# Another seven-product form for the second matmul of groups 1 to 5: four chained sums a side, products gathered in three banks

## Chip, cores and metric

The kernel runs on one core of one Trainium2 chip. The time is device time in microseconds of one execution; beside it stands the span, the time from the first to the last instruction in the profile of one execution. The core's engines are TensorE (PE in the profile; its weight loads are PEld), VectorE (DVE), ScalarE (ACT), GpSimd (POOL) and SyncE (SP, which here only issues DMAs).

## What is computed

The input is `q`, `k`, `v` of 4 batches, 8 heads, 768 positions and 64 channels. A linear attention with a decay for each head is worked out block by block. Its output, seen as 3072 tokens of 512 channels, goes through an MLP: a matmul with `w_in`, an exact GELU, a matmul with `w_out`.

```python
for b in range(nb):                                  # blocks of 64 positions
    intra = einsum('bhic,bhjc->bhij', qb, kb) * Dmask
    intra = einsum('bhij,bhjd->bhid', intra, vb)
    inter = einsum('bhid,bhde->bhie', qb * lam_pow, kv_state)
    out[:, :, sl] = intra + inter
    kv_state = lam_block * kv_state + einsum('bhsd,bhse->bhde', kb * rev_pow, vb)
h = x @ w_in                                         # 3072 x 512 by 512 x 2048
g = 0.5 * h * (1 + erf(h / sqrt(2)))
return g @ w_out                                     # 3072 x 2048 by 2048 x 512
```

## The kernel before

The 3072 tokens are worked on in six groups of 512, four chunks of 128 tokens each. For every group the attention gives `x_t`, the first matmul (`mm1`, L511 to L522) multiplies it with `w_in` into PSUM tiles `h_ps`, and ACT writes the GELU of each as bf16 into `g_t`, with the 2048 hidden channels on partitions in 16 slices `k` and the 512 tokens in the free dimension. The second matmul takes `g_t` and `w_out_t`, both bf16. Group 0 does it plainly (`mm2`, L526). Groups 1 to 5 do it in `blocks_by_seven` (L375): `g_t` is cut in two halves of the tokens (`lo`, `hi`) and two of the hidden channels (slices 0 to 7 and 8 to 15), `w_out_t` in two halves of the hidden channels and two of the output channels (B11, B12, B21, B22), and the 2 by 2 block product, eight products by definition, is made of seven.

The seven-product form before needs five sums of blocks of `w_out_t`, made once while group 0 runs (`w_out_sums`, L371, ten DVE instructions at L368), and five sums of blocks of `g_t` for each group (`g_sum`, L384, ten DVE instructions at L389, half of each issued inside the first matmul, blocks 10 to 14 of the group, the other half inside the second). Each product is worked out in two parts `u` of 128 tokens; one part is eight matmuls of 128 weights by 256 columns into one half of a PSUM tile of 128 x 2 x 256 f32 (L414). One such tile fills one PSUM bank. The products run in the order `m3 m4 m5 m2 m1 m6 m7`. Products 3 and 4 are copied to SBUF by ACT (L433, L443). DVE adds or subtracts the others with them (L452, L453, L465, L466, L484, L489, L498; in group 5 L482 and L495 by halves of 256 columns). Product 7 is added on top of product 1 in the same bank `r_ps`, and that bank is read after both halves of product 1 and again after product 7. In group 5 each half of `r_ps` is a tile of its own. The results are stored from `o0_sb` (the first two chunks) and `o1_sb` (the last two) by SP (`store`, L421).

PSUM tiles come from rings by tag: `mo` and `mh` have two banks each. `mh` also holds `h_ps`, and `mo` also holds the `kv_ps` of the attention.

The order is written by hand. A group of 1 to 5 is a list of 30 blocks, 16 of the first matmul and 14 of the second (L501), each of equal cost, and the steps of the attention for later groups are put in front of blocks by their number (`steps`, where `B` is one block, and `g + 26 * B` is block 26 of group `g`). Each engine runs its instructions in the order in which they were issued. The steps that fall among the last blocks of the second matmul are the two `empty_half` (L333, a DVE multiplication from the attention's PSUM to `x_t`; in groups 1 to 4, before blocks 26 and 28) and, in groups 1 to 3, four DMA transposes of `k` and `q` on SP's queue before block 26. Group 1 has more: a visit of the attention before block 20 that takes both banks of `mh`, a mask and states for it, and four ACT copies before block 23 (`reorder_states`, L229).

Of the kernel before, what the change touches and what calls it, by code (L numbers as in the profile page):

```python
# [8 lines left out]
F32 = mybir.dt.float32  # L9
BF16 = mybir.dt.bfloat16  # L10
ALU = mybir.AluOpType
# [4 lines left out]
def kernel(  # L16
# [10 lines left out]
    nc = tc.nc  # L27

    B, H, S, D = q.shape
    d_model, d_ff = moe_w_in.shape  # L30
# [21 lines left out]
    out_pool = ctx.enter_context(tc.tile_pool(name="outp", bufs=2))  # L52
# [36 lines left out]
    w_out_t = w_pool.tile([128, NK2, d_model], BF16)  # L89
# [58 lines left out]
    def bank(shape, dtype, tag, name):  # L148
        return ps.tile(shape, dtype, tag=tag, name=name, bufs=2 if tag in ("sc", "mh", "mo") else 1)
# [191 lines left out]
    def empty_outputs(c):  # L341
# [6 lines left out]
        else:  # L348
# [3 lines left out]
    KH = NK2 // 2  # L352
    DH = d_model // 2
    wsum = {}
    w_lo, w_hi = slice(0, KH), slice(KH, NK2)
    d_lo, d_hi = slice(0, DH), slice(DH, d_model)
    B11, B12, B21, B22 = ((w_lo, d_lo), (w_lo, d_hi), (w_hi, d_lo), (w_hi, d_hi))
    W_SUMS = {1: (B11, B22, ALU.add), 3: (B12, B22, ALU.subtract), 4: (B21, B11, ALU.subtract),
              6: (B11, B12, ALU.add), 7: (B21, B22, ALU.add)}

    def w_out_sum(i, half):

        if i not in wsum:
            wsum[i] = w_pool.tile([128, KH, DH], BF16, name=f"w_sum{i}")
        (ka, da), (kb, db), op = W_SUMS[i]
        n = KH // 2
        at = lambda ks: slice(ks.start + half * n, ks.start + (half + 1) * n)
        nc.vector.tensor_tensor(wsum[i][:, half * n:(half + 1) * n, :], w_out_t[:, at(ka), da], w_out_t[:, at(kb), db],  # L368
                                op=op)

    def w_out_sums():  # L371
        for i, half in [(6, 0), (6, 1), (7, 0), (1, 0), (3, 0), (4, 0), (7, 1), (1, 1), (3, 1), (4, 1)]:
            w_out_sum(i, half)

    def blocks_by_seven(g, g_t, first):  # L375

        last = g == NG - 1
        TH = M * C // 2
        lo, hi = slice(0, TH), slice(TH, 2 * TH)
        gsum = {}  # L380
        G_SUMS = {6: (0, hi, 0, lo, ALU.subtract), 1: (0, lo, KH, hi, ALU.add), 2: (0, hi, KH, hi, ALU.add),
                  5: (0, lo, KH, lo, ALU.add), 7: (KH, lo, KH, hi, ALU.subtract)}

        def g_sum(i, k):  # L384
            if i not in gsum:
                gsum[i] = sum_pool.tile([128, KH, TH], BF16, tag=f"g{i}", name=f"g_sum{i}")
            ka, ta, kb, tb, op = G_SUMS[i]
            ks = slice(k, k + n4)
            nc.vector.tensor_tensor(gsum[i][:, ks, :], g_t[:, ka + k:ka + k + n4, ta], g_t[:, kb + k:kb + k + n4, tb],  # L389
                                    op=op)  # L390

        n4 = KH // 2

        def with_sums(i, run):
            def both():
                run()
                if i in sums_at:
                    g_sum((5, 2, 1, 6, 7)[sums_at.index(i)], 0)
            return both

        sums_at = range(10, 15)
        blocks = [(with_sums(i, run), cost) for i, (run, cost) in enumerate(first)]

        left = {1: lambda k, t: gsum[1][:, k, t], 2: lambda k, t: gsum[2][:, k, t],
                3: lambda k, t: g_t[:, k, t], 4: lambda k, t: g_t[:, KH + k, TH + t.start:TH + t.stop],
                5: lambda k, t: gsum[5][:, k, t], 6: lambda k, t: gsum[6][:, k, t], 7: lambda k, t: gsum[7][:, k, t]}
        right = {2: lambda k: w_out_t[:, k, d_lo], 5: lambda k: w_out_t[:, KH + k, d_hi]}
        right.update({i: (lambda k, i=i: wsum[i][:, k, :]) for i in W_SUMS})

        banks, sb = {}, {}  # L410

        def product(i, u, o, begin):
            for k in range(KH):
                nc.tensor.matmul(o, left[i](k, slice(u * C, (u + 1) * C)), right[i](k),  # L414
                                 start=(begin and k == 0), stop=(k == KH - 1), skip_group_check=True)

        def tile_f(name):
            sb[name] = sum_pool.tile([128, 2, DH], F32, tag=f"f_{name}", name=f"f_{name}")
            return sb[name]

        def store(rows, us, cols):  # L421
            b = slice(rows * 2 + us.start, rows * 2 + us.stop)
            dst = out_r[g, :, b, cols]
            nc.sync.dma_start(dst, sb["o0" if rows == 0 else "o1"][:, us, cols])

        both, every = slice(0, 2), slice(0, d_model)

        def m3(u):
            if u == 0:
                banks["p"] = bank([128, 2, DH], F32, "mo", "p_ps")  # L430
            product(3, u, banks["p"][:, u, :], u == 0)
            if u == 1:
                nc.scalar.copy(tile_f("e"), banks["p"])  # L433
                g_sum(5, n4)

        def m4(u):
            if u == 0:
                banks["q"] = bank([128, 2, DH], F32, "mo", "q_ps")
            product(4, u, banks["q"][:, u, :], u == 0)
            if u == 0:  # L440
                g_sum(2, n4)
            else:
                nc.scalar.copy(tile_f("f"), banks["q"])  # L443

        def m5(u):
            if u == 0:
                banks["p5"] = bank([128, 2, DH], F32, "mo", "p5_ps")
                g_sum(1, n4)
            product(5, u, banks["p5"][:, u, :], u == 0)
            if u == 1:  # L450
                sb["o0"] = out_pool.tile([128, 2, d_model], F32, tag="o0", name="o0_sb", bufs=1)
                nc.vector.tensor_add(sb["o0"][:, :, d_hi], sb["e"], banks["p5"])  # L452
                nc.vector.tensor_sub(tile_f("x1"), sb["f"], banks["p5"])  # L453
                if last:
                    store(0, both, d_hi)

        def m2(u):
            if u == 0:
                banks["q2"] = bank([128, 2, DH], F32, "mo", "q2_ps")
            product(2, u, banks["q2"][:, u, :], u == 0)  # L460
            if u == 0:
                g_sum(6, n4)
            else:
                sb["o1"] = out_pool.tile([128, 2, d_model], F32, tag="o1", name="o1_sb", bufs=1)
                nc.vector.tensor_add(sb["o1"][:, :, d_lo], sb["f"], banks["q2"])  # L465
                nc.vector.tensor_sub(tile_f("x2"), sb["e"], banks["q2"])  # L466

        def m1(u):
            if u == 0:
                banks["s"] = bank([128, 2, DH], F32, "mh", "s_ps")  # L470
                if last:
                    banks["r"] = [bank([128, DH], F32, tag, "r_ps") for tag in ("mh", "t")]
                else:
                    r_ps = bank([128, 2, DH], F32, "mh", "r_ps")
                    banks["r"] = [r_ps[:, 0, :], r_ps[:, 1, :]]
                    banks["r_all"] = r_ps
            product(1, u, banks["r"][u], u == 0 or last)
            if u == 0:
                g_sum(7, n4)
            elif last:  # L480
                for w in range(2):
                    nc.vector.tensor_add(sb["x2"][:, w, :], sb["x2"][:, w, :], banks["r"][w])  # L482
            else:
                nc.vector.tensor_add(sb["x2"], sb["x2"], banks["r_all"])  # L484

        def m6(u):
            product(6, u, banks["s"][:, u, :], u == 0)
            if u == 1:
                nc.vector.tensor_add(sb["o1"][:, :, d_hi], sb["x2"], banks["s"])  # L489
                store(1, both, every)  # L490

        def m7(u):
            product(7, u, banks["r"][u], False)
            if last:
                nc.vector.tensor_add(sb["o0"][:, u, d_lo], sb["x1"][:, u, :], banks["r"][u])  # L495
                store(0, slice(u, u + 1), d_lo)
            elif u == 1:
                nc.vector.tensor_add(sb["o0"][:, :, d_lo], sb["x1"], banks["r_all"])  # L498
                store(0, both, every)

        blocks += [((lambda f=f, u=u: f(u)), KH * DH) for f in (m3, m4, m5, m2, m1, m6, m7) for u in range(2)]  # L501
        return blocks

    N1 = 19
# [79 lines left out]
    def early(n):  # L584
        live[n] = begin(n, early=True)
        return live[n]
# [10 lines left out]
    c = early(0)  # L597
# [7 lines left out]
    c = early(1)  # L605
# [48 lines left out]
    e = N1  # L654
# [22 lines left out]
    def at(when, run):  # L677
        todo.append((place(when), run))
# [103 lines left out]
    n = 2 * M  # L782
# [9 lines left out]
    for g in range(2, NG):  # L792
        n = (g + 1) * M
# [14 lines left out]
        w = g + (10 if g == 2 else 8) * B  # L808
# [7 lines left out]
    for g in range(1, NG - 2):  # L816
        n = (g + 2) * M
# [48 lines left out]
```

## Time and profile before

| what | us |
| --- | --- |
| median of three executions | 202.98 |
| lowest, highest of the three | 200.58, 205.71 |
| the profiled execution | 201.34 |
| its span | 199.6 |
| outside the span | 1.74 |
| second matmul, group 1 | 67.06 to 80.95 |
| second matmul, group 2 | 98.25 to 110.47 |
| second matmul, group 3 | 127.82 to 140.05 |
| second matmul, group 4 | 156.48 to 168.71 |
| second matmul, group 5 | 183.57 to 195.8 |
| busy DVE, ACT over the span | 120.4, 82.7 |

A row of the profile's groups reads: line, engine, operation, output<-input, shape, count, then busy time in us, mean duration of one in ns, and the engine's idle time before them with what ended it. A row of the timeline reads: start in us, duration in us, engine, line, operation, count, and in brackets the idle time before it with what ended it. A row of the chain of work that ended last reads: start in us, duration, engine and line. Matmuls overlap in the array: a chain of sixteen lasts 1.91 us in the timeline from its first start to its last modelled end, and the next chain starts 1.75 us after it.

### The profile page before, as it was taken

The page shows a single profiled execution, that of the slowest core. Times are in us where ns is not written, and L with a number is a line of the kernel's source. Part 1 is how long each engine was busy: PE and PEld are TensorE (multiplying, and loading weights), DVE is VectorE, ACT ScalarE, POOL GpSimd, SP SyncE. Part 2 cuts the span into 40 slices and gives each one's busy share as a digit, 9 for nine tenths or more (in the row PEclk, how much of TensorE's full clock was granted, in tenths as well). Part 3 has the DMA queues.
Part 4 walks back from the last instruction along what each step waited for, and adds up shares of the span by engine and source line. Part 5 has one row for each costly group of instructions (what it writes and reads, how often), then busy time and mean ns, then how long its engine had stood idle before and what let it go on. Part 6 is the DMA issues. An engine that isn't in the chain of part 4 may idle for free.

```text
span 199.6 us, 5998 instructions
## 1 busy us (share of the span) xinstructions
PE 191.0 (96%) x2625; PEld 142.9 (72%) x2636; DVE 120.4 (60%) x206; ACT 82.7 (41%) x149; POOL 110.5 (55%) x136
## 2 busy tenths in 40 slices
PE   7699999999999999999999989999999999999992
PEld 2388674455887788885688875688884788865881
DVE  3753507764473869694949658649638358341482
ACT  4964564234556413174520255520355410566200
POOL 8999973499969799993493497591400000000000
PEclk9999999999999999999999999999999999999999
DMA  5999999999999999999799799899700002300014
GB/s 115 148 174 175 200 204 206 153 216 150 130 220 149 151 142 136 118 209 233 72 84 153 234 68 127 90 110 122 234 8 3 3 0 80 134 0 3 0 53 158
DMA packets 102761, 24.76 MB, mean 124 GB/s; under 512 B 93264, under 2 KB 99920, under 8 KB 102736
## 3 DMA queue, kind: packets, MB, share of 16 engines
q0 software_dynamic: 81072, 13.38, 99.3%
q1 hardware_dynamic: 21664, 11.02, 26.6%
q8 instruction: 20, 0.33, 0.7%
q14 instruction: 5, 0.04, 0.1%
HBM read 27.27 MB, written 6.29 MB: 168 GB/s over the span
## 4 chain that ended last, share of the span: by engine, by line
PE 73%; DMA 10%; POOL 10%; DVE 4%; issue 1%; POOLq 0%; DVEq 0%
PE h_ps L518 35%; PE r_ps L414 8%; PE p_ps L414 8%; PE q_ps L414 8%; DMA q_t<-in_q_dram 6%; DMA w_out_t<-in_moe_w_out_dram 4%; PE s_ps L414 4%; POOL w_in_t L94 3%; PE o_ps L531 3%; POOL k_t L70 2%; POOL q_t L70 2%; POOL v_t L70 2%; PE o_ps L314 2%; POOL v_dec L160 1%; PE kv_ps L290 1%
## 5 line engine op out<-in xcount | busy, mean ns | idle before, releaser
L518 PE MATMUL h_ps<-x_t,w_in_t 128*128 128x256 bf16 (+3 forms) x648 | 87.5, 290 | 1.0 <-issue 0.6
L521 ACT ACTIVATE g_t<-h_ps 128x512 bf16<-128x512 f32 (+2 forms) x99 | 57.8, 584 | 72.6 <-PE h_ps L518 72.6
L518 PEld LDWEIGHTS <-w_in_t 128*128 128x128 bf16 x656 | 58.4, 98 | 23.8 <-issue 1.0
L389 DVE TENSOR_TENSOR g_sum<-g_t 128x1024 bf16<-128x1024 bf16 x50 | 33.4, 713 | 16.4 <-ACT g_t L521 16.4
L414 PEld LDWEIGHTS <-g_sum 128*128 128x128 bf16 x400 | 39.1, 98 | 4.8 <-issue 0.3
L160 POOL TENSOR_TENSOR v_dec<-v_t,lam_m 128x512 bf16<-128x512 bf16 x23 | 24.3, 1094 | 25.6 <-PE o_ps L326 14.8
L70 POOL DMA_DIRECT2D v_t<-in_v_dram x24 | 22.2, 927 | 3.1 <-DMA w_out_t<-in_moe_w_out_dram 1.7
L414 PE MATMUL r_ps<-w_sum,g_sum 128*128 128x256 bf16 x160 | 19.1, 273 | 0.1
L73 POOL DMA_DIRECT2D k_t<-in_k_dram x24 | 18.7, 799 | 0.0
L73 POOL DMA_DIRECT2D q_t<-in_q_dram x24 | 18.3, 788 | 0.0
L414 PEld LDWEIGHTS <-g_t 128*128 128x128 bf16 x160 | 15.6, 98 | 2.9
L531 PE MATMUL o_ps<-w_out_t,g_t 128*128 128x512 bf16 x61 | 14.5, 379 | 0.4 <-issue 0.3
L333 DVE TENSOR_TENSOR x_t<-o_ps,lam_q 128x512 bf16<-128x512 f32 x16 | 10.6, 683 | 3.9 <-PE o_ps L314 3.9
L70 POOL DMA_DIRECT2D k_t<-in_k_dram x12 | 11.2, 933 | 1.9 <-DMA w_out_t<-in_moe_w_out_dram 1.6
L70 POOL DMA_DIRECT2D q_t<-in_q_dram x12 | 10.9, 908 | 2.4 <-DMA w_out_t<-in_moe_w_out_dram 2.4
L531 PEld LDWEIGHTS <-g_t 128*128 128x128 bf16 x64 | 5.9, 98 | 6.3
L305 DVE TENSOR_TENSOR sc_m<-sc_ps,cmask_d 128x512 bf16<-128x512 f32 x16 | 10.3, 679 | 0.0
L452 DVE TENSOR_TENSOR o_sb<-f_e,p_ps 128x512 f32<-128x512 f32 x5 | 3.4, 686 | 11.0 <-issue 11.0
L582 PE MATMUL idle_ps<-idle 128*128 128x256 bf16 (+1 forms) x40 | 8.7, 353 | 1.2 <-DVE idle L107 1.2
L414 PE MATMUL p_ps<-w_out_t,g_sum 128*128 128x256 bf16 x80 | 9.6, 273 | 0.0
L414 PE MATMUL s_ps<-w_sum,g_sum 128*128 128x256 bf16 x80 | 9.6, 273 | 0.0
L414 PE MATMUL q_ps<-w_out_t,g_sum 128*128 128x256 bf16 x80 | 9.6, 273 | 0.0
(90 smaller groups left out, 192.2 us busy)
## 6 DMA issues: line engine op xcount, KB each, us to landing
out_dram<-o_sb SPq DMA_DIRECT2D x9, 512.0 KB, 4.9
v_t<-in_v_dram POOLq DMA_DIRECT2D x24, 128.0 KB, 5.6
w_out_t<-in_moe_w_out_dram POOLq DMA_DIRECT2D x4, 512.0 KB, 10.3
w_in_t<-in_moe_w_in_dram POOLq DMA_DIRECT2D x7, 256.0 KB, 7.3
k_t<-in_k_dram POOLq DMA_DIRECT2D x12, 128.0 KB, 6.5
q_t<-in_q_dram POOLq DMA_DIRECT2D x12, 128.0 KB, 6.8
k_t<-in_k_dram POOLq DMA_DIRECT2D x24, 64.0 KB, 4.8
q_t<-in_q_dram POOLq DMA_DIRECT2D x24, 64.0 KB, 5.0
```

The source lines that it names most:

```text
L70: nc.gpsimd.dma_start(raw[n, name], chunk_of(name, n))
L73: nc.gpsimd.dma_start(raw[n, name][:, r::2, :], chunk_of(name, n)[:, r * HP:(r + 1) * HP, :])
L94: nc.gpsimd.dma_start(w_in_t[:, :, f], w_in_r[:, :, f])
L160: eng.tensor_mul(c.v_dec, c.v, lam_m[:, :, None].to_broadcast((128, H, D)))
L305: nc.vector.tensor_mul(w.sc_m[:, hi], w.sc_ps[hi], cmask_d[:, None, None, :].to_broadcast((128, 2, HP, D)))
L333: nc.vector.tensor_mul(x[:, :, :, HALVES[t]], pairs[n].o_ps[t], lam_q[:, :, None, HALVES[t]].to_broadcast((128, HP, 2, D)))
L389: nc.vector.tensor_tensor(gsum[i][:, ks, :], g_t[:, ka + k:ka + k + n4, ta], g_t[:, kb + k:kb + k + n4, tb], op=op)
L414: nc.tensor.matmul(o, left[i](k, slice(u * C, (u + 1) * C)), right[i](k), start=(begin and k == 0), stop=(k == KH - 1), skip_group_check=True)
L518: nc.tensor.matmul(h_ps[:, k, :], w_in_t[:, ki, (kf + k) * 128:(kf + k + 1) * 128], x_t[:, ki, cols], start=(k == 0 and ki == 0), stop=(ki ...
L521: nc.scalar.activation(g_t[:, kf:kf + ks, cols], h_ps, ACT.Gelu)
L531: nc.tensor.matmul(om[io], g_t[:, kf, io * C:(io + 1) * C], w_out_t[:, kf, :], start=(kf == 0), stop=(kf == NK2 - 1))
L582: nc.tensor.matmul(idle_ps[0][:, :cols], idle[:, :128], idle[:, :cols], start=True, stop=True)
```

## The change

The seven products are those of another form. With A11 (slices 0 to 7, `lo`), A12 (slices 8 to 15, `lo`), A21 (slices 0 to 7, `hi`), A22 (slices 8 to 15, `hi`):

- sums of `g_t`: S1 = A21 + A22, S2 = S1 - A11, S3 = A11 - A21, S4 = A12 - S2, four instead of five; sums of `w_out_t`: T1 = B12 - B11, T2 = B22 - T1, T3 = B22 - B12, T4 = B21 - T2, four instead of five. Two of each read an earlier sum.
- products: P1 = A11 B11, P2 = A12 B21, P5 = S1 T1, P6 = S2 T2, P3 = S4 B22, P7 = S3 T3, P4 = A22 T4, in this order, still two parts of eight matmuls each.
- bank `a` (tag `mo`) holds P1, then P1 + P6, then P1 + P6 + P7, then P1 + P6 + P7 + P4. It is read after each: P1 by ACT (`p1`), P1 + P6 by ACT (`u2`), P1 + P6 + P7 by DVE in two halves, the last by ACT in two halves straight into `o1_sb`. Bank `b` (`mh`) holds P2, bank `c` (`mo`) holds P5, then P5 + P3.
- DVE adds for one group: seven of 512 columns (in group 5 two of them in halves) become two of 512 and two of 256. ACT copies: two of 512 become three of 512 and two of 256.
- `o0_sb` is stored after P3, block 25, and `o1_sb` after P4, block 29; before, both stores came in the last four blocks.

Core of the diff:

```diff
-    W_SUMS = {1: (B11, B22, ALU.add), 3: (B12, B22, ALU.subtract), 4: (B21, B11, ALU.subtract),
-              6: (B11, B12, ALU.add), 7: (B21, B22, ALU.add)}
+    W_SUMS = {1: (B12, B11), 2: (B22, 1), 3: (B22, B12), 4: (B21, 2)}
...
-        G_SUMS = {6: (0, hi, 0, lo, ALU.subtract), 1: (0, lo, KH, hi, ALU.add), 2: (0, hi, KH, hi, ALU.add),
-                  5: (0, lo, KH, lo, ALU.add), 7: (KH, lo, KH, hi, ALU.subtract)}
+        G_SUMS = {1: ((0, hi), (KH, hi), ALU.add), 2: (1, (0, lo), ALU.subtract),
+                  3: ((0, lo), (0, hi), ALU.subtract), 4: ((KH, lo), 2, ALU.subtract)}
...
-                    g_sum((5, 2, 1, 6, 7)[sums_at.index(i)], 0)
+                    g_sum((1, 2, 4, 3)[sums_at.index(i)], 0)
...
+        def m1(u):
+            if u == 0:
+                banks["a"] = bank([128, 2, DH], F32, "mo", "a_ps")
+                g_sum(1, n4)
+                g_sum(2, n4)
+            chain(1, "a", u, True)
+            if u == 1:
+                nc.scalar.copy(tile_f("p1"), banks["a"])
+        def m2(u):
+            if u == 0:
+                banks["b"] = bank([128, 2, DH], F32, "mh", "b_ps")
+                g_sum(4, n4)
+                g_sum(3, n4)
+            chain(2, "b", u, True)
+            if u == 1:
...
+                nc.vector.tensor_add(sb[0][:, :, d_lo], sb["p1"], banks["b"])
+        def m5(u):
...
+            chain(5, "c", u, True)
+            if u == 1:
+                nc.scalar.copy(tile_f("p5"), banks["c"])
+        def m6(u):
+            chain(6, "a", u)
+            if u == 1:
+                nc.scalar.copy(tile_f("u2"), banks["a"])
+        def m3(u):
+            chain(3, "c", u)
+            if u == 1:
+                nc.vector.tensor_add(sb[0][:, :, d_hi], sb["u2"], banks["c"])
+                store(0, both, every)
+        def m7(u):
+            chain(7, "a", u)
+            nc.vector.tensor_add(sb[1][:, u, d_hi], sb["p5"][:, u, :], banks["a"][:, u, :])
+            if last and u == 1:
+                store(1, both, d_hi)
+        def m4(u):
+            chain(4, "a", u)
+            nc.scalar.copy(sb[1][:, u, d_lo], banks["a"][:, u, :])
+            if last:
+                store(1, slice(u, u + 1), d_lo)
+            elif u == 1:
+                store(1, both, every)
...
-        blocks += [((lambda f=f, u=u: f(u)), KH * DH) for f in (m3, m4, m5, m2, m1, m6, m7) for u in range(2)]
+        blocks += [((lambda f=f, u=u: f(u)), KH * DH) for f in (m1, m2, m5, m6, m3, m7, m4) for u in range(2)]
```

More of the change, by code (lines that the diff above doesn't have):

```diff
@@ L364, in w_out_sum, with part @@
             wsum[i] = w_pool.tile([128, KH, DH], BF16, name=f"w_sum{i}")
-        (ka, da), (kb, db), op = W_SUMS[i]
         n = KH // 2
-        at = lambda ks: slice(ks.start + half * n, ks.start + (half + 1) * n)
-        nc.vector.tensor_tensor(wsum[i][:, half * n:(half + 1) * n, :], w_out_t[:, at(ka), da], w_out_t[:, at(kb), db],
-                                op=op)
+        ks = slice(half * n, (half + 1) * n)
+        def part(x):
+            return wsum[x][:, ks, :] if isinstance(x, int) else w_out_t[:, x[0].start + ks.start:x[0].start + ks.stop, x[1]]
+        nc.vector.tensor_sub(wsum[i][:, ks, :], *map(part, W_SUMS[i]))
     def w_out_sums():
-        for i, half in [(6, 0), (6, 1), (7, 0), (1, 0), (3, 0), (4, 0), (7, 1), (1, 1), (3, 1), (4, 1)]:
-            w_out_sum(i, half)
+        for half in range(2):
+            for i in (1, 2, 4, 3):
+                w_out_sum(i, half)
     def blocks_by_seven(g, g_t, first):
@@ L386, in g_sum, with part @@
                 gsum[i] = sum_pool.tile([128, KH, TH], BF16, tag=f"g{i}", name=f"g_sum{i}")
-            ka, ta, kb, tb, op = G_SUMS[i]
             ks = slice(k, k + n4)
-            nc.vector.tensor_tensor(gsum[i][:, ks, :], g_t[:, ka + k:ka + k + n4, ta], g_t[:, kb + k:kb + k + n4, tb],
-                                    op=op)
+            def part(x):
+                return gsum[x][:, ks, :] if isinstance(x, int) else g_t[:, x[0] + k:x[0] + k + n4, x[1]]
+            a, b, op = G_SUMS[i]
+            nc.vector.tensor_tensor(gsum[i][:, ks, :], part(a), part(b), op=op)
         n4 = KH // 2
@@ L397, in both @@
                 if i in sums_at:
-                    g_sum((5, 2, 1, 6, 7)[sums_at.index(i)], 0)
+                    g_sum((1, 2, 4, 3)[sums_at.index(i)], 0)
             return both
-        sums_at = range(10, 15)
+        sums_at = range(10, 14)
         blocks = [(with_sums(i, run), cost) for i, (run, cost) in enumerate(first)]
[L404 to L408, printed above, removed]
+        left = {1: lambda k, t: g_t[:, k, t], 2: lambda k, t: g_t[:, KH + k, t],
+                3: lambda k, t: gsum[4][:, k, t], 4: lambda k, t: g_t[:, KH + k, TH + t.start:TH + t.stop],
+                5: lambda k, t: gsum[1][:, k, t], 6: lambda k, t: gsum[2][:, k, t], 7: lambda k, t: gsum[3][:, k, t]}
+        right = {1: lambda k: w_out_t[:, k, d_lo], 2: lambda k: w_out_t[:, KH + k, d_lo],
+                 3: lambda k: w_out_t[:, KH + k, d_hi]}
+        right.update({i: (lambda k, j=j: wsum[j][:, k, :]) for i, j in ((4, 4), (5, 1), (6, 2), (7, 3))})
         banks, sb = {}, {}
@@ L423, in store, with chain @@
             dst = out_r[g, :, b, cols]
-            nc.sync.dma_start(dst, sb["o0" if rows == 0 else "o1"][:, us, cols])
+            nc.sync.dma_start(dst, sb[rows][:, us, cols])
         both, every = slice(0, 2), slice(0, d_model)
-        def m3(u):
+        def chain(i, bank_name, u, begin=False):
+            product(i, u, banks[bank_name][:, u, :], begin and u == 0)
+        def m1(u):
             if u == 0:
-                banks["p"] = bank([128, 2, DH], F32, "mo", "p_ps")
-            product(3, u, banks["p"][:, u, :], u == 0)
+                banks["a"] = bank([128, 2, DH], F32, "mo", "a_ps")
+                g_sum(1, n4)
+                g_sum(2, n4)
+            chain(1, "a", u, True)
@@ L432, in m3 @@
             if u == 1:
-                nc.scalar.copy(tile_f("e"), banks["p"])
-                g_sum(5, n4)
-        def m4(u):
+                nc.scalar.copy(tile_f("p1"), banks["a"])
+        def m2(u):
             if u == 0:
[L438 to L443, printed above, removed]
+                banks["b"] = bank([128, 2, DH], F32, "mh", "b_ps")
[3 more added lines that the diff above has]
+            if u == 1:
+                for r in range(2):
+                    sb[r] = out_pool.tile([128, 2, d_model], F32, tag=f"o{r}", name=f"o{r}_sb", bufs=1)
+                nc.vector.tensor_add(sb[0][:, :, d_lo], sb["p1"], banks["b"])
@@ L445, in m5 @@
         def m5(u):
             if u == 0:
-                banks["p5"] = bank([128, 2, DH], F32, "mo", "p5_ps")
-                g_sum(1, n4)
-            product(5, u, banks["p5"][:, u, :], u == 0)
+                banks["c"] = bank([128, 2, DH], F32, "mo", "c_ps")
+            chain(5, "c", u, True)
             if u == 1:
[L451 to L484, printed above, removed]
@@ L486, in m6 @@
+                nc.scalar.copy(tile_f("p5"), banks["c"])
         def m6(u):
-            product(6, u, banks["s"][:, u, :], u == 0)
+            chain(6, "a", u)
             if u == 1:
-                nc.vector.tensor_add(sb["o1"][:, :, d_hi], sb["x2"], banks["s"])
-                store(1, both, every)
[L492 to L499, printed above, removed]
```

## The prediction

> **What bounds the kernel now.** First the page's busy shares and groups of instructions:
>
> ```profile
> span 199.6 us, 5998 instructions
> PE 191.0 (96%) x2625; PEld 142.9 (72%) x2636; DVE 120.4 (60%) x206; ACT 82.7 (41%) x149; POOL 110.5 (55%) x136
> ...
> L414 PE MATMUL r_ps<-w_sum,g_sum 128*128 128x256 bf16 x160 | 19.1, 273 | 0.1
> ```
>
> PE is busy for 96% of the span, and the seven-product matmuls (L414, here those into `r_ps`) sat idle for 0.1 us ahead of 160 of them. DVE has 79 us to spare. A share is an average, so I read the stage itself next, in the chain of work that ended last, at the end of group 2's second matmul:
>
> ```profile
> 105.23 1.75 PE r_ps L414 x16
> 106.98 1.75 PE s_ps L414 x16
> 108.73 1.75 PE r_ps L414 x16
> 110.47 0.87 PE h_ps L518 x8
> ```
>
> Chains of sixteen follow each other every 1.75 us, 0.87 us for one half, and the next group's first matmul follows at once. From 98.25 to 110.47 are 12.22 us for seven chains, or seven times 1.75: no wait at all. Groups 3, 4 and 5 have the same length. Only group 1 has one: `s_ps` starts at 77.30, so `r_ps` could start at 79.05 and does at 79.30. So this stage is PE and nothing else. The change leaves PE its 112 matmuls in each group, hence it can gain 0.25 us there and what the tail gives, and lose whatever makes PE wait.
>
> **Work that is removed, at no effect.** Ten `g_sum` at 713 ns, two `w_sum` at 685 ns and, per group, seven adds against two of 680 ns and two of 420: 7.1 + 1.4 + 5 x (4.8 - 2.2) = 21 us less for DVE. ACT gets per group one copy more of 586 ns and two of 128x256. Neither engine set PE's start in groups 2 to 5. The cover is 12.2 us of PE per group, in which DVE was busy for 7.4 to 8.8 us. The `w_sum` ended at 38.4, while the chain of waits is on the load of a `q_t` until 41.39; if that cover were gone, they'd be worth 1.4 us.
>
> **Sums that read sums.** S2 and S4 must wait for the sum ahead of them. Such a pair on DVE, `mid` then `tmp` in group 1, starts 0.80 us apart instead of 0.60, so the four second halves take 0.8 + 0.8 + 0.6 + 0.7 = 2.9 us. In group 5 DVE could start them at 184.23; the last ends at 187.1, P5, the first to read one, starts at 183.57 + 3.5 = 187.07 and needs only the first. Cost zero.
>
> **Waits that are added.** The order of the built program shows which matmuls carry a wait. In each group the first matmul of m7's second half waits for DVE's read of the first half of bank `a`, the first of m4's first half for DVE's read of the second half, and the first of m4's second half for ACT's copy of the first. All are in one bank: PE may not write one half while the other is read. So PE and a reader take turns three times in a group, and PE has nothing else queued that could pass: m4 and the next group's matmuls stand behind in order. Before, bank `r_ps` was read after both halves, and in group 5 each half had its own tile. That is how the last rows of before look, with no turns taken:
>
> ```profile
> 185.15 1.91 PE L414 MATMUL q_ps<-w_sum,g_t 128*128 128x256 bf16 x16
> ...
> 187.15 0.59 ACT L443 COPY f_f<-q_ps 128x512 f32<-128x512 f32 x1 [1.17 <-PE q_ps L414]
> ...
> 192.14 1.91 PE L414 MATMUL s_ps<-w_sum,g_sum 128*128 128x256 bf16 x16
> ...
> 193.88 1.91 PE L414 MATMUL r_ps<-w_sum,g_sum 128*128 128x256 bf16 x16
> 194.09 0.69 DVE L489 TENSOR_TENSOR o_sb<-f_x,s_ps 128x512 f32<-128x512 f32 x1 [0.84 <-PE s_ps L414]
> 194.96 0.42 DVE L495 TENSOR_TENSOR o_sb<-f_x,r_ps 128x256 f32<-128x256 f32 x1 [0.18 <-PE r_ps L414]
> 195.83 0.42 DVE L495 TENSOR_TENSOR o_sb<-f_x,r_ps 128x256 f32<-128x256 f32 x1 [0.45 <-PE r_ps L414]
> ```
>
> The price of one turn comes from them. A chain ends 1.91 - 1.75 = 0.16 us after the next could have started (192.14 + 1.91 = 194.05). DVE starts 0.04 later (194.09) and reads 256 columns in 0.42. How fast PE restarts after DVE shows in group 1, together with how closely DVE's instructions follow each other:
>
> ```profile
> 78.57 0.68 DVE L484 TENSOR_TENSOR f_x<-f_x,r_ps 128x512 f32<-128x512 f32 x1
> 79.17 0.68 DVE L333 TENSOR_TENSOR x_t<-o_ps,lam_q 128x512 bf16<-128x512 f32 x1
> 79.30 1.91 PE L414 MATMUL r_ps<-w_sum,g_sum 128*128 128x256 bf16 x16
> 79.77 0.67 DVE L489 TENSOR_TENSOR o_sb<-f_x,s_ps 128x512 f32<-128x512 f32 x1
> ```
>
> L484 ends at 79.25 and PE starts at 79.30, 0.04 to 0.05 later; DVE starts an instruction every 0.60 us. So a turn with DVE costs 0.16 + 0.04 + 0.42 + 0.04 = 0.66 us. With ACT: 185.15 + 1.91 = 187.06, the copy starts 0.09 later; 128x256 from PSUM takes about 0.38 (four GELUs of that shape have a mean of 384 ns): 0.16 + 0.09 + 0.38 + 0.04 = 0.67 us.
>
> The first turn of groups 1 to 4 is longer, since two DVE instructions stand ahead of its read: the add after P3 and `empty_half` of block 26. With T the start of m7, the add starts at T + 0.20 (P3 drains), `empty_half` at T + 0.80, the read at T + 1.40. It ends at T + 1.82, PE starts at T + 1.86 instead of T + 0.87: 0.99 us. The `empty_half` of block 28 is queued behind the second read and costs nothing.
>
> Groups 1 to 4: 4 x (0.99 + 0.66 + 0.67) = 9.3. Group 5 has no `empty_half`: 0.66 + 0.66 + 0.67 = 2.0. Together 11.3 us.
>
> Bounds of a turn, which before never shows whole: the matmul's end is modelled, so without the 0.16 it is 0.50; with the 0.59 of a 512-column copy in place of 0.38 to 0.42 it is 0.88. Fifteen turns, plus the 4 x 0.33 of the queue, give 8.8 to 14.5. I take 11.3, since the 256-column rows are the operation itself.
>
> A rule of the Trainium skill speaks against this change: "PSUM — Partial Sum Buffer", section "PSUM bank collisions raise a hardware error", asks that accesses be guarded by bank and not by address, since two engines on one bank and quadrant collide even at other columns. By it the three waits can't be left out; no run here shows a collision.
>
> **Smaller terms.** Group 1: the 0.25 us stall goes, as DVE has less ahead of it. But its visit before block 20 takes both banks of `mh`, of which `b` is one. P2 ends at 70.55, the four sums, begun at 68.03, end at 70.9, DVE adds `b` from 70.81 to 71.50, and the visit's `kv_ps` matmuls, at 71.02 before, start at 71.54: 0.5 us lost. Net +0.25.
>
> SP: `o0_sb`'s store now stands ahead of the four transposes of block 26, and waits for the add after P3. In group 2 they were issued at 102.51 to 109.36; behind a store at about 108.3, the last goes out at 112.9 and lands 5.5 us later (the transposes' median; 8.4 at most), 121.3 at the worst. Their reader, the second visit of group 3, ran at 119.53, and group 2's own 2.3 us of turns come in between: 121.9. Cost zero, and in groups 1 and 3, where the readers stand as far off, too. POOL's loads keep their blocks.
>
> Tail: a last 256-column read and a 128 KB store end both kernels. Before, 512 KB were issued 1.5 us ahead of it; now 256 KB some 3 us ahead. DMA moved data from 195 to 198, the last store was issued at 196.3 and took about 2 us to land: between 0 and 0.7 us to gain, I take 0.2.
>
> **Sum.** 11.3 + 0.25 - 0.2 = 11.35. Against the profiled execution's 201.34 (span 199.6 and 1.74 around it) that is 212.7; against the median of 202.98, 1.64 higher, it is 214.3. I predict the middle, 213.5.
>
> **Rivals.**
> *Halves pass freely (not slower).* If a read of one half held only writes to that half, m7 would run through, m4's first half would start at T + 1.86 instead of T + 1.75, its second half without a wait: 4 x 0.11 + 0.25 - 0.2 = 0.5, so 201.8 (203.5 by the median), within 2%. It decides on whether the first matmul of m7's second half starts 0.87 us after m7 does. For it: the two halves share no column. Against: the built program has the wait. 7%.
> *The clock drops.* Three idle stretches a group could lower PE's granted clock. If it were half for the four blocks of m7 and m4, their 3.5 us would take 3.5 more, 5 x 3.5 = 17.5, giving 230. Against it: the granted clock is 0.999 over the whole span, with waits of 1.2 us (for `idle`) among it. 4%. The Trainium skill, "TensorE: Matmul & The Clock Gate", section "A second HAM failure mode: psum-queue depth-cycling", reports such a drop from short idles between banks; by that rule it would be 230, and the trace's 0.999 does not bear it out so far.
> *Turns as costed, at 8.8 to 14.5 in all:* 88%, the forecast. The last 1% is DVE's relief being worth more than the stage shows: faster, below 199.
>
> **Range and chances.** The low end is 8.8 - 0.5 on 201.34, rounded down for the scatter of the runs (200.58 to 205.71, 2.5%): 208. The high end is 14.5 + 0.5 on 202.98: 218. Left out are the rivals' 12% and a few per cent of scatter. The scatter is why about 2%, 4.1 us, is what a measurement of this kernel can tell from no change. Slower by more than that, past 207.0: the forecast and the clock, 0.92. Within 2%: 0.07. Faster: 0.01.
>
> **What would show it.** In the profile after: `a_ps` of m7's second half idle about 1 us before it with DVE's add (L477) as releaser, 0.66 in group 5; m4's halves 0.66 each, the second released by ACT's copy (L483); a second matmul of 14.5 us in groups 2 to 4 and 14.2 in group 5; DVE near 100 us busy; granted clock 0.999. The prediction is wrong if these stretches last 12.2 us, if PE's matmuls themselves get longer, or if `sc_ps` of a second visit waits for a transpose.

## The result and the profile after

| | before | after |
| --- | --- | --- |
| median, us | 202.62 (4 runs, 200.58 to 205.71) | 212.53 (4 runs, 212.31 to 213.74) |
| profiled execution, its span, us | 201.34, 199.6 | 212.67, 210.9 |
| second matmul, group 1, us | 14.20 | 16.52 |
| second matmul, groups 2 and 3, us | 12.23, 12.23 | 14.63, 14.62 |
| second matmul, group 4, us | 12.32 | 14.73 |
| second matmul, group 5, us | 12.39 | 14.68 |
| from PE's last end to the end of the span, us | 3.81 | 3.43 |

The kernel is slower: the ratio is 1.0536, with a 95% interval of 1.0442 to 1.063. It compares the means of the runs without the one of 205.71, which counts as a slow run, being over 1.5% above the fastest of its kernel. The stages are taken from PE's starts in the timeline, from the first matmul of the stage to the first one behind it (in group 5 to the last one's end); the chain of waits, which lets a piece begin where the one before ends, has the same starts some 0.17 us later.

The page of the changed kernel, its first lines:

```profile
span 210.9 us, 5991 instructions
## 1 busy us (share of the span) xinstructions
PE 193.6 (92%) x2625; PEld 143.2 (68%) x2636; DVE 103.1 (49%) x177; ACT 89.4 (42%) x164; POOL 110.6 (52%) x136
```

DVE does 17 us less than before, ACT 7 us more, and PE, with 2625 matmul records in both, went from 96% to 92% of a longer span. Whom PE waited for is in its waits (who waited, for whom, then us in total, times, longest):

```profile
PE a_ps L420 <- DVE o_sb L477: 6.7, 10, 0.9
PE a_ps L420 <- ACT o_sb L483: 2.8, 5, 0.8
...
PE kv_ps L290 <- DVE o_sb L455: 0.2, 1, 0.2
```

Fifteen waits on readers of bank `a`, three for each of five groups, 9.5 us of idle time: the same view of the kernel before has no row for a bank of the products. The timeline of group 3, with the loads and other queues left out, shows the turns one by one:

```profile
140.93 1.04 PE L420 MATMUL a_ps<-w_sum,g_sum 128*128 128x256 bf16 x8
141.20 0.69 DVE L472 TENSOR_TENSOR o_sb<-f_u,c_ps 128x512 f32<-128x512 f32 x1 [4.57 <-PE c_ps L420]
141.80 0.68 DVE L333 TENSOR_TENSOR x_t<-o_ps,lam_q 128x512 bf16<-128x512 f32 x1
...
142.41 0.41 DVE L477 TENSOR_TENSOR o_sb<-f_p,a_ps 128x256 f32<-128x256 f32 x1
...
142.87 1.03 PE L420 MATMUL a_ps<-w_sum,g_sum 128*128 128x256 bf16 x8 [0.90 <-DVE o_sb L477]
143.94 0.42 DVE L477 TENSOR_TENSOR o_sb<-f_p,a_ps 128x256 f32<-128x256 f32 x1 [1.12 <-PE a_ps L420]
...
144.41 1.03 PE L420 MATMUL a_ps<-w_sum,g_t 128*128 128x256 bf16 x8 [0.51 <-DVE o_sb L477]
...
145.53 0.37 ACT L483 COPY o_sb<-a_ps 128x256 f32<-128x256 f32 x1 [5.50 <-PE a_ps L420]
145.95 1.03 PE L420 MATMUL a_ps<-w_sum,g_t 128*128 128x256 bf16 x8 [0.50 <-ACT o_sb L483]
...
146.82 1.04 PE L506 MATMUL h_ps<-x_t,w_in_t 128*128 128x256 bf16 x8
```

The starts of PE are 1.94, 1.54, 1.54 and 0.87 us apart. Eight matmuls that wait for nobody take 0.87, so the turns cost 1.07, 0.67 and 0.67 and the last half nothing. The idle time in brackets is smaller by 0.16 to 0.17, as it begins at the modelled end of the last matmul: what the stage pays is the distance of starts, not the idle time. Group 5 pays 0.67, 0.68 and 0.95. Added up over the groups the second matmul grew by 2.32 + 2.40 + 2.39 + 2.41 + 2.29 = 11.8 us; the tail gave back 0.4 and the rest of the program 0.1, which leaves the 11.3 us between the spans. (That 0.1 is itself a balance: before has an idle stretch of 0.57 us at 115.5, in a first matmul, that the changed kernel hasn't, and the changed kernel has one of 0.27 us at 85.7 that before hasn't. Neither lies in a second matmul.)

### The profile page after: what moved, and what is told of

Read it like the earlier page. It is cut to its first block, busy times and chain, and to the rows that moved or that the text cites. A ratio compares the mean times of both kernels' runs of the same rounds, so it can differ in the third digit from the quotient of the medians.

```text
span 210.9 us, 5991 instructions
## 1 busy us (share of the span) xinstructions
PE 193.6 (92%) x2625; PEld 143.2 (68%) x2636; DVE 103.1 (49%) x177; ACT 89.4 (42%) x164; POOL 110.6 (52%) x136
## 4 chain that ended last, share of the span: by engine, by line
PE 69%; DMA 10%; POOL 9%; DVE 6%; issue 2%; ACT 1%; ACTq 0%; DVEq 0%; POOLq 0%
PE h_ps L506 32%; PE a_ps L420 15%; PE c_ps L420 8%; DMA q_t<-in_q_dram 6%; DMA w_out_t<-in_moe_w_out_dram 4%; PE b_ps L420 3%; POOL w_in_t L94 2%; PE o_ps L519 2%; DVE o_sb L477 2%; POOL k_t L70 2%; POOL q_t L70 2%; POOL v_t L70 2%; PE o_ps L314 2%; POOL v_dec L160 1%; PE kv_ps L290 1%
## 5 line engine op out<-in xcount | busy, mean ns | idle before, releaser
L420 PEld LDWEIGHTS <-g_sum 128*128 128x128 bf16 x320 | 31.2, 98 | 8.6 <-issue 5.0
L420 PEld LDWEIGHTS <-g_t 128*128 128x128 bf16 x240 | 23.4, 98 | 10.8 <-issue 7.1
L395 DVE TENSOR_TENSOR g_sum<-g_t 128x1024 bf16<-128x1024 bf16 x20 | 14.5, 727 | 18.8 <-ACT g_t L509 18.8
L420 PE MATMUL a_ps<-w_sum,g_sum 128*128 128x256 bf16 x160 | 19.9, 272 | 4.1 <-DVE o_sb L477 4.1
L483 ACT COPY o_sb<-a_ps 128x256 f32<-128x256 f32 x10 | 3.7, 373 | 32.5 <-PE a_ps L420 32.5
L420 PE MATMUL a_ps<-w_sum,g_t 128*128 128x256 bf16 x80 | 10.3, 272 | 5.3 <-ACT o_sb L483 2.8
L472 DVE TENSOR_TENSOR o_sb<-f_u,c_ps 128x512 f32<-128x512 f32 x5 | 3.4, 688 | 21.5 <-PE c_ps L420 21.5
L519 PEld LDWEIGHTS <-g_t 128*128 128x128 bf16 x64 | 5.9, 97 | 6.3
L704 DVE COPY seen<-o_ps 128x4 f32<-128x4 f32 (+1 forms) x7 | 1.1, 164 | 17.7 <-PE o_ps L314 17.7
```

The costliest lines, as they stand in the source:

```text
L395: nc.vector.tensor_tensor(gsum[i][:, ks, :], part(a), part(b), op=op)
L519: nc.tensor.matmul(om[io], g_t[:, kf, io * C:(io + 1) * C], w_out_t[:, kf, :], start=(kf == 0), stop=(kf == NK2 - 1))
```

## The experiments

The theory: PE and the reader of bank `a` take turns, each turn costs the drain, the read and the restart, and it costs that only because PE has nothing else to do. The rivals: the new form is slow for something else it brings (sums that read sums, more ACT copies, the store ahead of the transposes), or reading a bank in the middle of its accumulation costs in itself. Each ratio below is to runs of the kernel before taken beside the experiment (median 202.64 us; 201.59 for the last two), and each stage is that of group 3 where nothing else is said.

**Each half of `a` in a bank of its own.** All the arithmetic stays; `c` moves to the tag `mh`, and ACT copies P1 and P1 + P6 by halves.

```diff
-            product(i, u, banks[bank_name][:, u, :], begin and u == 0)
+            product(i, u, banks["a"][u], begin)          # for bank "a"
-                banks["a"] = bank([128, 2, DH], F32, "mo", "a_ps")
+                banks["a"] = [bank([128, DH], F32, "mo", "a_ps") for _ in range(2)]
-                banks["c"] = bank([128, 2, DH], F32, "mo", "c_ps")
+                banks["c"] = bank([128, 2, DH], F32, "mh", "c_ps")
...
-            if u == 1:
-                nc.scalar.copy(tile_f("p1"), banks["a"])
+            nc.scalar.copy(sb["p1"][:, u, :], banks["a"][u])     # and the same for "u2"
```

> The same form, sums, products and order, but each half of bank a is a tile in a bank of its own (c moves to mh, and ACT copies P1 and P1+P6 by halves). Theory of the turns: m7's second half no longer waits for the read of the first, m4's first half waits 0.11 us in groups 1 to 4 and its second half not at all. Second matmul of groups 2 to 4: 12.2 to 12.4 us instead of 14.62; time within 1% of the kernel before. Rival, the form itself is slow (sums that read sums, more ACT copies, a store ahead of the transposes): all of that is still there, so 14.6 us and 212.

Measured: 202.42 us, ratio to the kernel before 0.9992 (0.9952 to 1.0031). Group 3 in the timeline, products 7 and 4:

```profile
137.02 1.91 PE L420 MATMUL a_ps<-w_sum,g_sum 128*128 128x256 bf16 x16
138.96 1.91 PE L420 MATMUL a_ps<-w_sum,g_t 128*128 128x256 bf16 x16
140.70 1.04 PE L510 MATMUL h_ps<-x_t,w_in_t 128*128 128x256 bf16 x8
```

The two halves of each product run through as one chain of sixteen. P4 starts 1.94 after P7 instead of 1.75: the first half's read, queued behind two DVE instructions, is 0.19 late, where 0.11 was expected. The stage is 12.42 us. The whole loss is gone while the new form is still all there, so the form isn't slow for anything else. (In group 1 `c`, now in `mh`, waited 0.24 us for a reader of the visit.)

**The same bank, the gaps filled.** The banks and the reads of `a` stay; the order of the blocks is another. Two things move with it: the second halves of S3 and S4 are issued with P5 instead of P2, and `o0_sb` is stored after P2, which now comes near the end, instead of after P3 (in group 5, half after each). So this kernel no longer has the store ahead of the transposes; the one with two banks still has it.

```diff
-for f in (m1, m2, m5, m6, m3, m7, m4) for u in range(2)]
+for f, u in ((m1, 0), (m1, 1), (m5, 0), (m5, 1), (m6, 0), (m6, 1), (m3, 0),
+             (m7, 0), (m3, 1), (m7, 1), (m2, 0), (m4, 0), (m2, 1), (m4, 1))]
```

> The same banks, reads and waits, another order: m1, m5, m6, then halves in turn m3, m7, m3, m7, m2, m4, m2, m4, so that a chain into another bank stands in each of the gaps. Theory of the turns: a turn takes 0.66 to 0.85 us and a chain in the gap 0.87, so every wait is met before PE comes to it: 12.2 to 12.3 us in groups 2 to 5, time 201 to 203, no slower than the kernel before, perhaps 0.3 us faster by group 1 and the tail. Rival, reading a bank in the middle of its accumulation costs in itself wherever it stands: 14.6 us, 212.

Measured: 202.59 us, ratio 1.0017 (0.9972 to 1.0062). The timeline of group 3 around the first turn:

```profile
134.21 1.03 PE L420 MATMUL a_ps<-w_sum,g_sum 128*128 128x256 bf16 x8
135.08 1.04 PE L420 MATMUL c_ps<-w_out_t,g_sum 128*128 128x256 bf16 x8
...
135.34 0.42 DVE L479 TENSOR_TENSOR o_sb<-f_p,a_ps 128x256 f32<-128x256 f32 x1 [3.58 <-issue]
...
135.96 1.04 PE L420 MATMUL a_ps<-w_sum,g_sum 128*128 128x256 bf16 x8
```

DVE reads the first half of `a` from 135.34 to 135.76, while PE writes `c`; when PE returns to `a` at 135.96 the read is over, and PE's starts stay 0.87 to 0.89 us apart. The stage is 12.24 us. A read amid the accumulation is free where another bank's chain covers it. In group 1, where P5 now comes second, PE waited 0.39 us for its `g_sum` instead. Neither this kernel nor the one with two banks is faster than the kernel before by anything that can be measured, though DVE is busy for 106 and 104 us in them against 120.

**One instruction less ahead of the first read.**

```diff
-        ... (g + 26 * B, empty_half, done, 0) ...
+        ... (g + 24 * B, empty_half, done, 0) ...      # and the same in group 1
```

> Changed kernel with the first empty_half of groups 1 to 4 issued before block 24 instead of 26, so that it isn't queued between DVE's add after P3 and the first read of m7. Theory: the first turn falls from 0.99 to 0.66, the second matmul of groups 2 to 4 from 14.62 to 14.29 us, the time by 1.3 us to about 211.2. Rival, the queue ahead of the read doesn't matter: 14.62 and 212.5.

Measured: 211.9 us, ratio 1.0478 (1.0425 to 1.0531). PE's part of the timeline of group 3:

```profile
140.77 1.04 PE L420 MATMUL a_ps<-w_sum,g_sum 128*128 128x256 bf16 x8
142.32 1.03 PE L420 MATMUL a_ps<-w_sum,g_sum 128*128 128x256 bf16 x8 [0.51 <-DVE o_sb L477]
143.86 1.03 PE L420 MATMUL a_ps<-w_sum,g_t 128*128 128x256 bf16 x8 [0.51 <-DVE o_sb L477]
145.40 1.03 PE L420 MATMUL a_ps<-w_sum,g_t 128*128 128x256 bf16 x8 [0.50 <-ACT o_sb L483]
146.27 1.04 PE L506 MATMUL h_ps<-x_t,w_in_t 128*128 128x256 bf16 x8
```

The first turn is now like the other two, 1.55 us from start to start, and the stage 14.24: the queue on DVE ahead of the read was worth 0.4 us a group. On the time as a whole 1.3 us were expected and 0.6 were seen; this interval overlaps that of the changed kernel, so the time alone would not have shown it. (In the profile group 1 began 0.9 us later than in the changed kernel, before any of the edited steps; its granted clock was 0.53 from 8 to 10 us and 0.61 from 10 to 12, against 1.00 in the changed kernel. That this is the cause of the late start isn't shown.)

**Fewer and longer turns.**

```diff
-            nc.vector.tensor_add(sb[1][:, u, d_hi], sb["p5"][:, u, :], banks["a"][:, u, :])
+            if u == 1:
+                nc.vector.tensor_add(sb[1][:, :, d_hi], sb["p5"], banks["a"])
...
+            elif u == 1:                                 # groups 1 to 4
+                nc.scalar.copy(sb[1][:, :, d_lo], banks["a"])
```

> Changed kernel in which P1+P6+P7 is read by one DVE add of 512 columns after both halves, and in groups 1 to 4 the last sum by one ACT copy of 512. One turn is left of three, with a longer read: 0.16 + 0.04 + 0.69 + 0.04 = 0.93 us. Theory: 13.15 us in groups 2 to 4, group 5 keeps a second turn of 0.67; time 212.5 - 4 x (2.40 - 0.93) - 0.4 = 206.2. Rival, the loss goes by the columns read and not by the number of turns: 14.6 us and 212.

Measured: 205.98 us, ratio 1.0189 (1.014 to 1.0239). Group 3:

```profile
137.67 1.91 PE L420 MATMUL a_ps<-w_sum,g_sum 128*128 128x256 bf16 x16
140.36 1.91 PE L420 MATMUL a_ps<-w_sum,g_t 128*128 128x256 bf16 x16 [0.78 <-DVE o_sb L478]
142.10 1.04 PE L508 MATMUL h_ps<-x_t,w_in_t 128*128 128x256 bf16 x8
```

One turn of 2.69 - 1.75 = 0.94 us is left, against 0.93 expected; its read started at 139.62, when the two DVE instructions ahead of it were done. The same columns are read; what counts is how often PE and a reader change places. Reading by halves, which looks like the finer overlap, is the worse choice inside one bank: with the waits of this program the first half's read can't overlap the second half's matmuls.

**A turn in the old form.** The kernel before, with one read moved.

```diff
             product(1, u, banks["r"][u], u == 0 or last)
+            if not last:
+                nc.vector.tensor_add(sb["x2"][:, u, :], sb["x2"][:, u, :], banks["r"][u])
...
-            else:
-                nc.vector.tensor_add(sb["x2"], sb["x2"], banks["r_all"])
```

> Kernel before, old form, with one edit: in groups 1 to 4 product 1 is added to x2 by halves, each half read as soon as it is done, while the other half of the same bank is still to be written. Theory of the turns: one turn appears in a form that had none. In groups 2 to 4 DVE is busy with L466 until its next start 0.93 us after m1 begins plus 0.42 of read and 0.04 of restart, so 0.94 us: second matmul 13.16 us instead of 12.22; in group 1, where DVE is later, 1.5 to 1.8; time about 202.6 + 3 x 0.94 + 1.7 = 207.1. Rival, the loss belongs to the new form: 12.22 and 202.6, since the arithmetic and the columns read are the same.

Measured: 206.49 us, ratio 1.0271 (1.0157 to 1.0385). Group 2 in PE's timeline:

```profile
106.31 1.04 PE L414 MATMUL r_ps<-w_sum,g_sum 128*128 128x256 bf16 x8
108.48 1.03 PE L414 MATMUL r_ps<-w_sum,g_sum 128*128 128x256 bf16 x8 [1.14 <-DVE f_x L479]
109.35 1.91 PE L414 MATMUL s_ps<-w_sum,g_sum 128*128 128x256 bf16 x16
```

So the old form loses as well once a bank is read by halves. The turn is 2.17 - 0.87 = 1.30 us where 0.94 was expected. The read started at 108.01: L466, which writes the `x2` that is read, began at 107.22, and the read had to wait for its end, 0.79 us later instead of the 0.60 of independent instructions; L466 in turn began 0.91 after the half's first matmul and not 0.75, since I had taken that from the chain of waits and not from the timeline. (The 0.93 in the expectation is a slip: its 0.94 comes from a read that starts 0.75 + 0.60 = 1.35 after the half's first matmul.) In group 1 the turn was 1.97 us where 1.5 to 1.8 was expected.

**Six more small ACT instructions**, in the first 20 us of the changed kernel, for the 0.95 us of the third turn in group 5:

```diff
-    nc.scalar.activation(warm, pos, ACT.Gelu)
+    for _ in range(7):
+        nc.scalar.activation(warm, pos, ACT.Gelu)
```

> Changed kernel with six more tiny activations on ACT in the first 20 us. Question: ACT's copy after m4's first half in group 5 started 0.34 us after PE's end in the changed kernel and in the one with the earlier empty_half, but 0.04 to 0.08 in all other places. If the lag belongs to a place in ACT's instruction stream (code loading), six instructions more move it to six instructions earlier, a GELU near 190 us, and the turn takes 0.67. If it belongs to the turn (its waits, the store), it stays. Time within 0.5 us of the changed kernel either way.

Measured: 212.95 us in its one run. PE's longest wait for the copy was 0.5 us instead of 0.8, so the lag left the turn. It did not turn up six instructions earlier, as a fixed place in ACT's stream would have it: ACT's idle time ahead of each GELU near 190 us was 0.27 to 0.28 us, as in the changed kernel. Where it went can't be seen.

## Why the prediction was right, point by point

- **The stage is PE alone.** Right: the kernels with two banks and with filled gaps take 14 to 17 us off DVE and stay at the time of before.
- **Three turns a group at 0.99, 0.66 and 0.67.** Measured 1.07, 0.67 and 0.67. ACT's turn came out in each of its parts: copy 0.09 after PE's end, 0.37 long, PE 0.05 later. The term that was a little small is the first: DVE's add after P3 started 0.27 us after m7 did, not 0.20 (P3 ended at 141.09, the add began 0.11 later, not 0.04). The 0.04 was one row of several: in the kernel before, L452 began at 188.90, 0.09 after its bank's last matmul ended.
- **The queue of two DVE instructions ahead of the first read**, 0.33: with one of them gone, by the earlier `empty_half`, the turn fell by 0.40 to the length of the other two.
- **Group 5, 2.0:** 2.29, of which 0.28 is the late ACT copy, which nothing in the profile of before could show.
- **Group 1, +0.25 on top of the turns:** its `kv_ps` matmuls did wait for the read of `b`, 0.38 us from start to start instead of 0.5 (idle 0.16), and the old 0.25 stall went; the group grew by 2.32 in all, so the extra on top of its turns (1.07, 0.67 and 0.63) was nil.
- **Tail, -0.2 between 0 and -0.7:** -0.38.
- **Sums that read sums, SP's order, POOL:** zero, as said. The second halves of the four sums took 2.7 us in group 1 (67.97 to 70.70), and PE never waited for one, nor `sc_ps` for a transpose, though in group 3 the transposes went out from 142.46 on, behind the store.
- **DVE's relief, 21 us:** 17.3. The sum of durations was too large, as neighbouring DVE instructions overlap: mean 0.69, but a start every 0.60. It lies off the path, so the time doesn't feel it.
- **11.35 us on 201.34 gave 212.7** against the profiled execution of 212.67. That the two agree to 0.03 us is luck: for the five second matmuls 11.3 + 0.25 = 11.55 us were forecast and 11.8 measured, and the tail with 0.4 instead of 0.2 and the rest of the program with 0.1 instead of nothing made up for it. That each turn is there, with its releaser and within 0.1 us of its price but for the late copy, is not. The shift to 213.5, for a median 1.64 above the profiled run, wasn't needed: the runs after scatter by 1.4 us, those before by 5.
- **Rivals.** Halves that pass freely: refuted, for this program, by the fifteen waits. The clock: it did not drop at the turns. Asked by windows, the changed kernel's granted clock is 1.00 in the last blocks of all five groups (from 108 to 116 us and from 139 to 147 in groups 2 and 3), with three idle stretches of 0.5 to 0.9 us in each. The 0.997 of the whole span comes from its last 1.9 us, where it was 0.71 and PE had ended. What the Trainium skill ("TensorE: Matmul & The Clock Gate", section "A second HAM failure mode: psum-queue depth-cycling") reports of short idles between banks did not set in here.
- **The rule on banks.** The Trainium skill ("PSUM — Partial Sum Buffer", section "PSUM bank collisions raise a hardware error") asks for such waits by bank. The advice of the Trainium skill (the same page, section "Summary: rules for kernel authors") to read a different bank while a matmul runs is what the two repaired kernels do, at 12.42 and 12.24 us a stage against 14.62. Whether the chip itself would bear a read of one half beside a write of the other, no run here shows.

## What to carry to other kernels

Before saving an engine that has time to spare, ask which bank the busy engine must come back to: each return to a bank that is being read costs the drain, the whole read with what is queued ahead of it, and the restart, 0.67 us here for 256 columns, whatever columns are touched. Put another bank's chain of at least that length in the gap, or give the halves banks of their own; if neither is possible, read once and whole rather than twice by halves. And where a saving lies off the path, as 17 us of DVE did here, a repaired version ends at the old time, not below it.

## What the runs showed of the hardware that was not expected

- After a wait PE loses nothing beyond the wait: it restarted 0.04 to 0.05 us after the reader's end, and the eight matmuls behind took 0.87 us from start to start of the next chain, as in a run without waits.
- In four kernels ACT began one copy of group 5 late, 0.35 to 0.37 us after PE's end, where the same copy began within 0.1 us in group 3. In the changed kernel and in the one with the earlier `empty_half` it is the copy after m4's first half. In the one with filled gaps it is that copy too, while PE, which had ended the half at 194.57, writes `b`:

```profile
194.92 0.37 ACT L485 COPY o_sb<-a_ps 128x256 f32<-128x256 f32 x1 [4.94 <-PE a_ps L420]
```

  In the one with two banks it is the copy of `c` (189.86 to 190.23), where PE waits for nothing. So the lag is not one of the turn, though the turn pays for it: in group 5 of the changed kernel it is the step from 0.67 to 0.95 us.

```profile
204.62 1.03 PE L420 MATMUL a_ps<-w_sum,g_t 128*128 128x256 bf16 x8 [0.51 <-DVE o_sb L477]
...
206.01 0.37 ACT L483 COPY o_sb<-a_ps 128x256 f32<-128x256 f32 x1 [5.39 <-PE a_ps L420]
206.44 1.03 PE L420 MATMUL a_ps<-w_sum,g_t 128*128 128x256 bf16 x8 [0.78 <-ACT o_sb L483]
```

  With six more ACT instructions early on, or with four fewer copies, no copy of group 5 was late. That fits a lag that depends on what ACT did before, but what it waits for is not shown by the profile and stays open.
